# Reordering TensorE's opening and the block sums of an attention-plus-FFN kernel

## The chip, the cores and the metric

The kernel runs on one core of a Trainium2 chip. The metric is the device time of one execution in microseconds (us). Times of a kernel are the median over its executions; a profile is one execution with the hardware profiler, and its "span" runs from the first to the last instruction (mostly 1.8 to 2.0 us shorter than the device time of the same execution).

## The reference

```python
def _attn_ref(q, k, v, E, F):                      # q, k, v: 8 x 8 x 1024 x 64
    k_proj = np.einsum('ks,bhsd->bhkd', E, k)      # 64 projected positions
    v_proj = np.einsum('ks,bhsd->bhkd', F, v)
    scores = scale * np.matmul(q, k_proj.transpose(0, 1, 3, 2))
    attn = softmax(scores)                         # written out with max, exp, sum in the original
    return np.matmul(attn, v_proj)
# then, with x = the attention output as 8192 x 512:
h = x @ w_in                                       # 512 -> 2048
g = h * (1.0 / (1.0 + np.exp(-1.702 * h)))
return g @ w_out                                   # 2048 -> 512
```

## The kernel before

The 8192 rows are done in 16 blocks of 512 (two blocks for each batch). A block is a first FFN part (matmuls of line L399), a second FFN part (L423), and between their matmuls, at places named by `at(block, slot, ...)`, pieces of attention for later blocks. Batch 0 has no FFN to hide in and is done in the open, in the "opening". The parts that matter:

```python
    def v_piece(p, cp):                            # opening: v's projection of two heads
        v_ps = proj0(1, 2 * p, 2)                  # L177, 8 matmuls
        for r, t in ((LO, p % 2), (HI, 1 - p % 2)):
            cp(vx0[p][r, t, :D], v_ps[r, t])       # L203, two copies on the engine given
    ...
    def kv_out(b):                                 # after a batch's projections (L169)
        def go():
            ps = kvps.pop(b)
            k_b = att.tile([KP, H, D], BF16, name="k_b")
            nc.vector.tensor_copy(k_b, ps[LO])     # L217
            nc.sync.dma_start_transpose(out=kts[b % 2], in_=k_b...)   # L218, makes kt
            v_out(b, ps)                           # L211, two copies to vq
        return go
    ...
    def sums(h):                                   # softmax sums of block h, L296
        def go():
            d_ps = [ps_x.tile([P, TB], F32, name="x_ps") for _ in range(2)]
            ... 8 matmuls ...
            for e in range(2):
                nc.vector.reciprocal(rden[:, e, :], d_ps[e])          # L299
        return go

    def spread(h):                                 # reciprocals to DRAM, then to all partitions
        def go():
            nc.sync.dma_start(out=rdr, in_=...)                       # L306
            for e, r in enumerate((LO, HI)):
                nc.sync.dma_start(out=rbc[h][r], in_=rdr[...]...)     # L309
        return go

    def values(h, u):                              # attention's output of block h
        def go():
            n_ps = [ps_x.tile([P, TB], F32, name="x_ps") for _ in range(2)]
            ... 8 matmuls ...
            for i in range(2):                     # L331, frees the two x_ps tiles
                nc.vector.tensor_tensor(x_of(h)[...], n_ps[i], rbc[h][...], op=ALU.mult)
        return go
    ...
    at(2, 3, proj(2), kv_out(2), sums(3), spread(3))
    at(2, O + 6, proj(3), kv_out(3), scores(5, 1), sums(4), spread(4))
```

The `x_ps` tiles are four in all. `sums(4)` takes the two that `values(3, 0)` used, so it can start only when block 3's first two multiplies are done, and these need block 3's `rbc`.

The softmax here doesn't subtract the row's maximum and nothing guards it: scores larger than these inputs give would overflow.

Of the kernel before, what the change touches and what calls it, by code (L numbers as in the profile page):

```python
# [17 lines left out]
def kernel(ctx, tc, q, k, v, E, F,  # L18
                                                     moe_w_in, moe_w_out, out):
    nc = tc.nc  # L20
# [88 lines left out]
    LO, HI = slice(0, KP), slice(KP, P)  # L109
# [22 lines left out]
    def f_tile(shape, dt=F32):  # L132
        return ps_f.tile(shape, dt, name="f_ps")

    def warm(n, f=False, z=zeros):
        w_ps = f_tile([P, TB]) if f else ps_x.tile([P, TB], F32, name="x_ps")
        for _ in range(n):
            nc.tensor.matmul(w_ps, z[:, :P], z, start=True, stop=True)  # L138
# [19 lines left out]
    def eft(j, cols=slice(0, 2 * KP)):  # L158
        return efts[j // (J // 2)][:, j % (J // 2), cols]
# [4 lines left out]
    def proj(b):  # L164
        def go():
            kvps[b] = f_tile([P, H, D])
            for j in range(J):
                for e, r in enumerate((LO, HI)):
                    nc.tensor.matmul(kvps[b][r], eft(j, slice(e * KP, (e + 1) * KP)),  # L169
                                     (kt, vt)[e][b][:, :, j, :],  # L170
                                     start=(j == 0), stop=(j == J - 1))
        return go

    def proj0(e, h0, n):
        ps = f_tile([P, n, D])
        for j in range(J):
            nc.tensor.matmul(ps, ffs[:, j].rearrange("s i k -> s (i k)") if e else eft(j), (kt, vt)[e][0][:, h0:h0 + n, j, :],  # L177
                             start=(j == 0), stop=(j == J - 1))
        return ps
# [16 lines left out]
    def vx_of(b, p):  # L196
        return vx1[:, 2 * p:2 * p + 2] if b == 1 else vx0[p]

    def v_piece(p, cp):

        v_ps = proj0(1, 2 * p, 2)
        for r, t in ((LO, p % 2), (HI, 1 - p % 2)):
            cp(vx0[p][r, t, :D], v_ps[r, t])  # L203

    def v_out(b, v_ps):
        vv = v_ps[HI].rearrange("k (u x) d -> k u x d", x=4)
        for r, xs_ in ((LO, X_LO), (HI, X_HI)):
            if b == 1:
                vx = vx1[r, :, :D].rearrange("k (u x) d -> k u x d", x=4)
                nc.vector.tensor_copy(vx[:, :, xs_], vv[:, :, xs_])  # L210
            nc.vector.tensor_copy(vqs[b % 2][r].rearrange("k (u e) d -> k u e d", e=2), vv[:, :, xs_, :])  # L211

    def kv_out(b):
        def go():
            ps = kvps.pop(b)
            k_b = att.tile([KP, H, D], BF16, name="k_b")
            nc.vector.tensor_copy(k_b, ps[LO])  # L217
            nc.sync.dma_start_transpose(out=kts[b % 2], in_=k_b.rearrange("k h d -> k (h d)"))  # L218
            v_out(b, ps)
        return go  # L220
# [11 lines left out]
    def q_tr(g):  # L232
        def go():
            if 0 not in qT:
                qT[0] = att.tile([P, J, HP, P], BF16, name="qT")
            t_ps = f_tile([P, 2, HP, P], BF16)
            for jj in range(2):
                for h in range(H):
                    r = h % 2 * D
                    nc.tensor.transpose(t_ps[r:r + D, jj, h // 2, :], qt[0][:, h, 2 * g + jj, :], ident)  # L240
            nc.vector.tensor_copy(qT[0][:, 2 * g:2 * g + 2], t_ps)
        return go

    def q_dma(b, j0=0, n=J):
        def go():
            if j0 == 0:
                qT[b] = att.tile([P, J, HP, P], BF16, name="qT")
            nc.sync.dma_start_transpose(out=qT[b][:, j0:j0 + n].rearrange("r j p s -> r (j p) s"),
                                        in_=qt[b][:, j0:j0 + n].rearrange("s j h d -> s (j h d)"))
        return go  # L250
# [32 lines left out]
    def x_of(h):  # L283
        if h not in xT:
            xT[h] = att.tile([P, KC, TB], BF16, name="xT", bufs=3)
        return xT[h]

    def sums(h):


        def go():
            d_ps = [ps_x.tile([P, TB], F32, name="x_ps") for _ in range(2)]
            for p in range(HP):
                for e in range(2):
                    r = HI if (p + e) % 2 else LO
                    nc.tensor.matmul(d_ps[e][32 * p:32 * p + 32], ones[r, :32], expT[h][r, p, :], start=True, stop=True)  # L296
            rden = att.tile([P, 2, TB], F32, name="rden", bufs=1)
            for e in range(2):
                nc.vector.reciprocal(rden[:, e, :], d_ps[e])  # L299
            rdens[h] = rden  # L300
        return go

    def spread(h):
        def go():
            rdr = dram.tile([HP, 2, TB], F32, name="rdr")
            nc.sync.dma_start(out=rdr, in_=rdens.pop(h)[0:P:32])  # L306
            rbc[h] = att.tile([P, HP, TB], F32, name="rbc")
            for e, r in enumerate((LO, HI)):
                nc.sync.dma_start(out=rbc[h][r], in_=rdr[None, :, e, :].to_broadcast([D, HP, TB]))  # L309
        return go  # L310
# [30 lines left out]
    def sums0(half):  # L341
        d_ps = ps_x.tile([P, HP, 2, 2], F32, name="x_ps")
        for p in range(HP):
            for i in range(2):
                t = 2 * half + i
                nc.tensor.matmul(d_ps[:, p, i, :], expT[0][:, p, t * P:(t + 1) * P],
                                 vx_of(0, p)[:, :, D:].rearrange("r t o -> r (t o)"), start=True, stop=True)
        nc.vector.reciprocal(rd0[:, half], d_ps)

    def tok0(p, a):  # L350
        n_ps = (f_tile if a else lambda s: ps_x.tile(s, F32, name="x_ps"))([P, 2, 2, D])
        for i in range(2):
            t = 2 * a + i
            nc.tensor.matmul(n_ps[:, i].rearrange("s t d -> s (t d)"),
                             expT[0][:, p, t * P:(t + 1) * P], vx_of(0, p)[:, :, :D], start=True, stop=True)
        if p not in xs:
            xs[p] = work.tile([P, 2, 2, 2, D], BF16, name="x0_sb", bufs=4)
        nc.vector.tensor_tensor(xs[p][:, a], n_ps, rd0[:, a, p, :, :, None].to_broadcast([P, 2, 2, D]), op=ALU.mult)

    def x_tr0(p, a, n, cp):  # L360
        n_ps = ps_x.tile([P, 2 * n, P], BF16, name="x_ps")
        for t in range(2 * n):
            nc.tensor.transpose(n_ps[:, t, :], xs[p][:, a + t // 2, t % 2].rearrange("s t d -> s (t d)"), ident)
        cp(x_of(0)[:, p, a * TB // 2:(a + n) * TB // 2], n_ps.rearrange("r t s -> r (t s)"))
# [69 lines left out]
    def at(j, slot, *fs):  # L434
        fill.setdefault((j, slot), []).extend(fs)
# [7 lines left out]
    DV, AC = nc.vector.tensor_copy, nc.scalar.copy  # L443
# [7 lines left out]
    gelu_table()  # L451
    v_piece(0, DV)
    sums0(0)
    tok0(0, 0)
    v_piece(1, DV)
    tok0(1, 0)
    sums0(1)
    v_piece(2, DV)
    tok0(0, 1)
    tok0(1, 1)  # L460
    v_piece(3, AC)
    tok0(2, 0)
    tok0(2, 1)
    x_tr0(0, 0, 2, AC)
    warm(1, True)
    tok0(3, 0)
    tok0(3, 1)
    x_tr0(1, 0, 2, AC)
    warm(1, True)
    x_tr0(2, 0, 2, DV)  # L470
    x_tr0(3, 0, 1, AC)
    x_tr0(3, 1, 1, DV)
    at(0, 13, q_tr(2))
    at(0, 15, q_tr(3))
    for u in range(2):
# [2 lines left out]
    for p in range(HP):  # L478
        at(0, Q + (4, 6, 9, 11)[p], tok(1, p, 0), tok(1, p, 1))
        at(0, Q + (6, 9, 11, 12)[p], x_tr(1, p, 0), x_tr(1, p, 1))  # L480
    at(1, 1, q_dma(1, 0, JB))
    at(1, 5, proj(1), kv_out(1), q_dma(1, JB, JB))
    for u in range(2):
        at(1, O, scores(2, u, None, u > 0))
# [6 lines left out]
        at(1, O + 6, scores(3, u, None, u > 0))  # L491
    at(1, O + 6, gelu_table)
    at(1, O + 4, q_dma(2))
    at(2, 3, proj(2), kv_out(2), sums(3), spread(3))
    at(2, O, q_dma(3))
    at(2, O + 3, scores(5, 0))
    at(2, O + 6, proj(3), kv_out(3), scores(5, 1), sums(4), spread(4))
    at(2, O + 7, gelu_table)
    for b in range(4, B):
# [66 lines left out]
```

## Time and profile before

| what | number | where from |
|---|---|---|
| device time | 509.6 us (508.96 to 509.95, 3 runs) | the first runs of the kernel before |
| device time of the profiled execution | 511.27 us | its record |
| span of the profile | 509.5 us | page |
| TensorE busy | 98% of the span | page |
| first FFN matmul starts | 23.47 us | TensorE's timeline |
| first landing of a piece of k | 9.54 us | the record of transfers |
| block 3's multiplies start | 119.17 us | VectorE's timeline |
| block 5's second scores, which block 4's sums follow | 119.40 us | TensorE's timeline |

The scores at 119.40 us are `scores(5, 1)` of the line `at(2, O + 6, ...)`, so block 5's, and block 4's sums come right behind them. The prediction and the expectations call them block 4's scores; nothing in the working hangs on the name. "The scores" below are these.

How to read the lines: a timeline line is start, duration, engine, source line, operation, out<-in, shapes and a count; in brackets it has the idle time of the engine ahead of it and what ended it. A line of the table of waits is: who waited <- for what: us in total, how often, the longest. The ends of matmuls are modelled (eight sums of before, listed with 386 ns each, start and give way to FFN within 0.35 us, 93.12 to 93.47), so distances between starts are used below. TensorE waits little (98% busy), and only its waits can be won. A landing is the time at which a transfer has arrived whole; a PSUM tile (`f_ps`, `x_ps`) is what matmuls write and another engine reads. In before, a matmul that takes such a tile again is listed as waiting for the reader: `PE x_ps L296 <- DVE xT L331: 0.2, 1, 0.2`.

### The profile page before, as it was taken

The page shows a single profiled execution, that of the slowest core. Times are in us where ns is not written, and L with a number is a line of the kernel's source. Part 1 is how long each engine was busy: PE and PEld are TensorE (multiplying, and loading weights), DVE is VectorE, ACT ScalarE, POOL GpSimd, SP SyncE. Part 2 cuts the span into 40 slices and gives each one's busy share as a digit, 9 for nine tenths or more (in the row PEclk, how much of TensorE's full clock was granted, in tenths as well). Part 3 has the DMA queues.
Part 4 walks back from the last instruction along what each step waited for, and adds up shares of the span by engine and source line. Part 5 has one row for each costly group of instructions (what it writes and reads, how often), then busy time and mean ns, then how long its engine had stood idle before and what let it go on. Part 6 is the DMA issues. An engine that isn't in the chain of part 4 may idle for free.

```text
span 509.5 us, 7096 instructions
## 1 busy us (share of the span) xinstructions
PE 501.5 (98%) x3034; PEld 227.2 (45%) x3034; DVE 156.2 (31%) x208; ACT 261.3 (51%) x426; POOL 77.8 (15%) x97
## 2 busy tenths in 40 slices
PE   7899999999999999999999999999999999999997
PEld 3644445444444444444444444444444444444444
DVE  4513204606261623216161331616214161611000
ACT  1565473654637355471746637374563737244351
POOL 6452150510600510041000510000000000000000
PEclk9999999999999999999999999999999999999999
DMA  9999999999799999499938979090603205050202
GB/s 164 200 202 207 195 160 175 213 202 136 137 216 268 132 153 205 130 153 93 239 55 214 104 116 233 13 241 1 172 0 74 93 7 160 1 167 0 84 0 82
DMA packets 124711, 68.76 MB, mean 135 GB/s; under 512 B 90580, under 2 KB 115540, under 8 KB 122760
## 3 DMA queue, kind: packets, MB, share of 16 engines
q0 software_dynamic: 83376, 29.37, 52.5%
q1 hardware_dynamic: 41224, 38.69, 30.8%
q8 instruction: 23, 0.38, 0.3%
q10 hardware_dynamic: 80, 0.26, 0.2%
q14 instruction: 8, 0.07, 0.0%
HBM read 72.88 MB, written 16.99 MB: 176 GB/s over the span
## 4 chain that ended last, share of the span: by engine, by line
PE 90%; DMA 6%; DVE 2%; POOL 1%; issue 0%; SPq 0%; ACT 0%; DVEq 0%; POOLq 0%
PE f_ps L399 41%; PE f_ps L423 41%; DMA v_sb<-in_v_dram 3%; DMA rbc<-rdr 2%; PE f_ps L169 2%; PE f_ps L258 1%; DVE rden L299 1%; PE x_ps L258 1%; DMA rdr<-rden 1%; PE f_ps L415 1%; PE x_ps L296 1%; POOL k_sb L57 0%; POOL v_sb L57 0%; PE x_ps L371 0%; PE x_ps L386 0%
## 5 line engine op out<-in xcount | busy, mean ns | idle before, releaser
L423 PE MATMUL f_ps<-w_out_sb,gT 128*128 128x512 bf16 x1008 | 226.7, 379 | 0.0
L399 PE MATMUL f_ps<-xT,w_in_sb 128*128 128x512 bf16 (+1 forms) x1032 | 224.4, 377 | 0.0
L401 ACT ACTIVATE gT<-f_ps 128x512 bf16<-128x512 f32 (+1 forms) x258 | 150.4, 594 | 61.4 <-PE f_ps L399 61.1
L399 PEld LDWEIGHTS <-w_in_sb 128*128 128x128 bf16 x1032 | 100.6, 98 | 119.8 <-issue 0.6
L423 PEld LDWEIGHTS <-gT 128*128 128x128 bf16 x1008 | 95.8, 98 | 121.7 <-issue 11.6
L426 ACT COPY o_sb<-f_ps 128x512 f32<-128x512 f32 x63 | 37.0, 587 | 131.6 <-PE f_ps L423 121.8
L331 DVE TENSOR_TENSOR xT<-x_ps,rbc 128x512 bf16<-128x512 f32 x52 | 33.3, 684 | 219.2 <-PE x_ps L258 115.3
L299 DVE RECIPROCAL rden<-x_ps 128x512 f32<-128x512 f32 x26 | 85.3, 3322 | 9.2 <-PE x_ps L296 9.2
L70 POOL DMA_DIRECT2D q_sb<-in_q_dram x48 | 42.1, 901 | 152.6 <-DMA qT<-q_sb 128.2
L277 ACT ACTIVATE expT<-f_ps 128x512 bf16<-128x512 f32 (+1 forms) x54 | 28.5, 580 | 29.4 <-PE f_ps L258 29.3
L277 ACT ACT_TABLE_LOAD x13 | 16.7, 1283 | 4.7 <-PE f_ps L258 4.5
L281 ACT ACT_TABLE_LOAD x14 | 18.0, 1283 | 0.3
L57 POOL DMA_DIRECT2D k_sb<-in_k_dram x10 | 8.5, 848 | 48.4 <-PE f_ps L169 46.3
L217 DVE CAST k_b<-f_ps 64x512 bf16<-64x512 f32 x7 | 4.8, 682 | 34.9 <-PE f_ps L169 34.9
L169 PE MATMUL f_ps<-k_sb,eft 128*64 128x512 bf16 x56 | 13.4, 382 | 0.0
L169 PE MATMUL f_ps<-v_sb,eft 128*64 128x512 bf16 x56 | 13.4, 382 | 0.0
L417 DVE COPY o_sb<-f_ps 128x256 f32<-128x256 f32 (+1 forms) x2 | 0.7, 358 | 37.3 <-issue 36.9
L138 PE MATMUL x_ps<-zeros 128*128 128x512 bf16 (+1 forms) x20 | 9.2, 589 | 1.5 <-DVE zeros L115 1.5
L258 PE MATMUL x_ps<-expT,vq 64*32 64x512 bf16 x208 | 10.2, 378 | 0.0
L258 PE MATMUL f_ps<-qT,kt 64*32 64x512 bf16 x200 | 10.2, 386 | 0.0
L57 POOL DMA_DIRECT2D v_sb<-in_v_dram x11 | 9.0, 822 | 7.9 <-DMA q_sb<-in_q_dram 4.3
L169 PEld LDWEIGHTS <-eft 128*64 128x64 bf16 x112 | 5.7, 109 | 7.3 <-issue 3.0
(75 smaller groups left out, 126.5 us busy)
## 6 DMA issues: line engine op xcount, KB each, us to landing
out_dram<-o_sb SPq DMA_DIRECT2D x15, 1024.0 KB
rbc<-rdr SPq DMA_DIRECT2D x26, 512.0 KB
k_sb<-in_k_dram POOLq DMA_DIRECT2D x7, 1024.0 KB, 13.4
v_sb<-in_v_dram POOLq DMA_DIRECT2D x7, 1024.0 KB, 17.6
q_sb<-in_q_dram POOLq DMA_DIRECT2D x48, 128.0 KB, 5.8
w_in_sb<-in_moe_w_in_dram POOLq DMA_DIRECT2D x8, 256.0 KB, 11.7
w_out_sb<-in_moe_w_out_dram POOLq DMA_DIRECT2D x4, 512.0 KB, 14.7
q_even<-in_q_dram POOLq DMA_DIRECT2D x2, 512.0 KB, 11.7
```

The source lines that it names most:

```text
L57: nc.gpsimd.dma_start(out=dst[b][:, h:h + n, js:js + jn], in_=sv[:, h:h + n, js:js + jn])
L70: nc.gpsimd.dma_start(out=qt[b][:, j], in_=qv[:, j])
L169: nc.tensor.matmul(kvps[b][r], eft(j, slice(e * KP, (e + 1) * KP)), (kt, vt)[e][b][:, :, j, :], start=(j == 0), stop=(j == J - 1))
L258: nc.tensor.matmul(outs[i][r.start + c:r.start + c + w], lhsTs[i][ri, c:c + w], rhss[i][ri], start=True, stop=True)
L277: nc.scalar.activation(expT[h][:, 2 * u + i, ts], s_ps[i], AF.Exp, scale=scale)
L281: nc.scalar.preload_act_table(AF.Gelu_apprx_sigmoid)
L299: nc.vector.reciprocal(rden[:, e, :], d_ps[e])
L331: nc.vector.tensor_tensor(x_of(h)[:, 2 * u + i, :], n_ps[i], rbc[h][:, 2 * u + i, :], op=ALU.mult)
L399: nc.tensor.matmul(h_ps, w_in_sb[:, kc, fc * P:(fc + 1) * P], xT[j][:, kc, ts], start=(kc == 0), stop=(kc == KC - 1))
L401: nc.scalar.activation(gts[j][:, fc, ts], h_ps, AF.Gelu_apprx_sigmoid)
L423: nc.tensor.matmul(o_ps[n], gts[j][:, fc, n * P:(n + 1) * P], w_out_sb[:, fc, :], start=(fc == 0), stop=(fc == FC - 1))
L426: nc.scalar.copy(osb[j][:, n, :], o_ps.pop(n))
```

## The change

The intent: in the opening, TensorE shall not stand right behind a copy that it needs; in block 2, block 3's sums shall come ahead of batch 2's projections, so that their reciprocals start earlier. In before a reciprocal of 128x512 from PSUM took VectorE 3322 ns on average of 26, a multiply of the same size 684, which is why the order on VectorE matters. The diff, whole:

```diff
-    def kv_out(b):
+    def kv_out(b, cp=nc.vector.tensor_copy):
...
-            nc.vector.tensor_copy(k_b, ps[LO])
+            cp(k_b, ps[LO])
...
     v_piece(0, DV)
     sums0(0)
+    v_piece(1, DV)
     tok0(0, 0)
-    v_piece(1, DV)
+    sums0(1)
     tok0(1, 0)
-    sums0(1)
     v_piece(2, DV)
     tok0(0, 1)
     tok0(1, 1)
-    v_piece(3, AC)
+    warm(1, True)
     tok0(2, 0)
     tok0(2, 1)
     x_tr0(0, 0, 2, AC)
-    warm(1, True)
+    v_piece(3, AC)
+    x_tr0(1, 0, 2, AC)
     tok0(3, 0)
     tok0(3, 1)
-    x_tr0(1, 0, 2, AC)
     warm(1, True)
-    x_tr0(2, 0, 2, DV)
-    x_tr0(3, 0, 1, AC)
-    x_tr0(3, 1, 1, DV)
+    x_tr0(2, 0, 2, AC)
+    x_tr0(3, 0, 1, DV)
+    x_tr0(3, 1, 1, AC)
...
-    at(2, 3, proj(2), kv_out(2), sums(3), spread(3))
+    at(2, 3, sums(3), proj(2), kv_out(2, nc.scalar.copy), spread(3))
```

`DV` and `AC` are the copies of VectorE and ScalarE, `tok0` is half-block values, `x_tr0` transposes them, `warm` is a filler matmul.

## The prediction

> **What bounds the kernel now.** I read the page first, then the table of TensorE's waits over the whole span, then TensorE's timeline in the opening and around block 2, and last VectorE's and SyncE's timelines beside them. The busy line (busy us, share of the span, instructions) comes first:
>
> ```profile
> PE 501.5 (98%) x3034; PEld 227.2 (45%) x3034; DVE 156.2 (31%) x208; ACT 261.3 (51%) x426; POOL 77.8 (15%) x97
> ```
>
> TensorE is busy for 98% of 509.5 us and the change removes no matmul, so it can win only idle time of TensorE. The table of waits (us in total, times, longest) shows how little of it the change can touch:
>
> ```profile
> PE x_ps L354 <- DVE vx L203: 0.9, 2, 0.6
> PE f_ps L177 <- DMA v_sb<-in_v_dram: 0.5, 1, 0.5
> PE x_ps L296 <- DVE xT L331: 0.2, 1, 0.2
> ```
>
> The first row is what the change's title speaks of: half-block values (L354) waiting for the copies of v's projections (L203). Two later rows matter as much. In TensorE's timeline of the opening (start, duration, what, and in brackets the idle time before) they stand so:
>
> ```profile
> 16.93 0.62 PE L177 MATMUL f_ps<-v_sb,ffs 128*128 128x128 bf16 x8
> ...
> 18.10 0.29 PE L354 MATMUL x_ps<-vx,expT 128*128 128x128 bf16 x2 [0.37 <-DVE vx L203]
> ...
> 19.40 0.29 PE L354 MATMUL x_ps<-vx,expT 128*128 128x128 bf16 x2 [0.56 <-DVE vx L203]
> ...
> 21.09 0.62 PE L177 MATMUL f_ps<-v_sb,ffs 128*128 128x128 bf16 x8 [0.52 <-DMA v_sb<-in_v_dram]
> ...
> 22.23 0.27 PE L354 MATMUL x_ps<-vx,expT 128*128 128x128 bf16 x2
> ...
> 23.47 10.64 PE L399 MATMUL f_ps<-xT,w_in_sb 128*128 128x256 bf16 x56
> ```
>
> After both copy waits TensorE still stands 0.52 us at 21.09 for the last quarter of v, whose transfer lands at 21.04. So the opening is set by that landing and by what must follow it, and the two copy waits lie before it, in slack. ScalarE and VectorE show what follows:
>
> ```profile
> 21.75 0.43 ACT L203 CAST vx<-f_ps 64x64 bf16<-64x64 f32 x2 [1.96 <-PE f_ps L177]
> ```
> ```profile
> 22.88 0.41 DVE L358 TENSOR_TENSOR x_sb<-f_ps,rd 128x256 bf16<-128x256 f32 x1
> ```
>
> The third row of the table is block 4's sums, at the end of block 2's second FFN part:
>
> ```profile
> 119.40 0.41 PE L258 MATMUL f_ps<-qT,kt 64*32 64x512 bf16 x8
> 119.92 0.37 PE L296 MATMUL x_ps<-expT,ones 64*32 64x512 bf16 x1
> 120.52 0.41 PE L296 MATMUL x_ps<-expT,ones 64*32 64x512 bf16 x7 [0.22 <-DVE xT L331]
> 120.86 1.90 PE L423 MATMUL f_ps<-w_out_sb,gT 128*128 128x512 bf16 x8
> ```
>
> Elsewhere eight scores are followed after 0.23 us by eight sums (138.22 to 138.45), and eight sums after 0.35 us by FFN matmuls (93.12 to 93.47). Here 119.40 to 120.86 is 1.46 us where 0.58 would do: **0.88 us** are lost, though the table lists 0.2. The sums need PSUM tiles that block 3's multiplies (L331) still hold, and those came late:
>
> ```profile
> 94.88 6.57 DVE L299 RECIPROCAL rden<-x_ps 128x512 f32<-128x512 f32 x2
> 119.17 2.48 DVE L331 TENSOR_TENSOR xT<-x_ps,rbc 128x512 bf16<-128x512 f32 x4 [17.73 <-DMA rbc<-rdr]
> ```
> ```profile
> 101.47 0.62 SPq L306 DMA_DIRECT2D rdr<-rden  x1
> 106.16 1.32 SPq L309 DMA_DIRECT2D rbc<-rdr  x2
> ```
>
> Two reciprocals until 101.44, a store to DRAM, 4.7 us to its landing, two broadcasts landing at 116.8 and 119.08, then the multiplies.
>
> [...] the second sums matmul starts 0.60 us after the first and only 0.22 is called idle, so I work from starts. [...] Here eight 128-column projections take 16.93 to 17.38, 56 ns each, and FFN groups of four follow every 0.86 us; moving them changes no cost. [...] The store of 16 KB took 4.7 us here and 1.9 at 129.78[...].
>
> **The change, part by part.** *1. Projections, sums and half-block values.* A projection can be used 1.17 us after its first matmul with VectorE's copies (16.93 to 18.10; 18.23 to 19.40), 1.14 with ScalarE's (21.09 to 22.23). The pieces on TensorE: projection 0.45, sums 0.21, a pair of values matmuls 0.12, four transposes 0.23, a filler matmul 0.23. Replayed in the new order: v0 at 16.93; sums 17.38; v1 17.59 to 18.04; values of pair 0 at 18.10, a wait of 0.06; second sums, whose last tile needs the exponential that ends at 18.49, until 18.60; values of pair 1 when v1's copies are done, at 18.87 (VectorE runs them 18.35 to 18.81, behind a reciprocal). v2 then starts at 18.99 instead of 19.73: **0.74 us gained at this point**, and v2's copies, queued behind two multiplies and a reciprocal on VectorE, end at about 20.24. Pair 2's values go at 20.30, its transposes of pair 0 by 20.9, and then TensorE meets the landing at 21.04. The whole 0.74 ends as more waiting; v3 starts at 21.09 as before.
>
> From there the necessary chain is v3, copies 21.75 to 22.18, pair 3's values 22.23, two multiplies (22.54 to 22.96, 22.88 to 23.29), transposes at 23.35, FFN at 23.47. In the old order the 0.68 us between v3's end (21.55) and 22.23 were filled exactly: values of pair 2 0.22, transposes 0.23, filler 0.23. The new order has moved these three ahead of v3 and leaves one set of transposes, 0.23: 0.45 us of open wait for the copies replace useful work, and pair 3 starts no sooner. Then values 0.22, filler 0.23, transposes of pair 2 from 22.68, pair 3's first half at 23.02 and second half at 23.35 after its multiply, FFN 23.47: the same. What the copies' new engines change is small: pair 2's copy ends at about 23.68 instead of 23.74, so the third FFN matmul starts at 23.73 instead of 23.79. Gain **0.06 us**.
>
> *2. Block 3's sums ahead of batch 2's projections.* The sums matmuls move from 93.12 to 91.28, and the reciprocals need not stand behind the copies of k and v (93.26 to 94.88). With 0.45 us from last matmul to reader (92.81 to 93.26) the reciprocals start at 91.31 + 0.45 = 91.76 instead of 94.88: 3.12 us earlier, and end at 98.33. The store lands 4.7 us later at 103.0, the broadcasts' second one at 103.7 + 12.2 = 115.9. To be in time for the sums at 119.63 it must land by 119.63 - 0.05 - 1.29 (first two multiplies, 119.17 to 120.46) = 118.3. It does by 2.4 us. So the **0.88 us** are gained whole.
>
> *3. k's copy to ScalarE.* ScalarE is idle from 91.98 to 94.54 in this stage and the copy (0.6 us, at about 93.6) fits; its transfer of kt moves from 93.97 to about 94.2, read at 105.66. Nothing on the path.
>
> Sum: 509.6 - 0.88 - 0.06 = 508.7 us.
>
> **Rivals.** *A: the copies' waits are worth what the table says.* Then 0.9 in the opening, perhaps also the 0.5, and with 0.88 the time is about 507.3 to 507.8. For it: the title's intent. Against: the landing at 21.04 does not move, since GpSimd issues it at 7.06 whatever TensorE does. *B: the held PSUM tile.* v's copies of batch 2 now stand behind the reciprocals, so the projections' tile is held until 98.33 + 0.87 = 99.2 instead of 94.84. Were it the fourth FFN group's, due at 93.47 + 3 x 0.863 = 96.1, TensorE would lose about 3 us (512). The instruction order of the built program speaks against it: the VectorE wait has moved from the fourth group after the projections to the ninth, due at 100.4, 1.2 us later than needed. *C: the broadcast is bound by the loads around it.* Loads of the next batch land from 104.7 to 122.3 in the same engines. If the store lands only when k's load is done, about 105, 1 us is left of the 3.1, enough by a hair; if nothing of it is left, the gain is 0.06 us (509.5). *D: the last quarter of v lands earlier in runs without this delay* (the earlier quarters came 1.3 us apart, this one 2.4). Then the old order could start FFN some 0.3 us sooner, and the new one, tied by its longer VectorE queue, only 0.1: about 508.9.
>
> **Range and chances.** I give the whole 0.88 about four chances in five. The three runs before spread over 1 us (508.96 to 509.95), which is as large as the gain, so the range is 507.9 to 509.5. Two per cent is 10 us; nothing here comes near it, either way: faster 0.01, same 0.98, slower 0.01.
>
> **What would show it.** Right: the waits table loses the L296 row; the store of block 3 issues near 98.4, its multiplies start near 116, and from block 4's scores to the next FFN takes 0.6 us; FFN starts within 0.1 us of 23.47; at pair 3's values a wait of about 0.4 for ScalarE's copies appears, beside waits for VectorE's of about 0.3 and 0.4 earlier. Wrong: FFN starting before 23.2 with the landing unmoved (A); an FFN matmul near 100 waiting for v's copies (B); the multiplies still after 118.3 (C).

Why the store took 4.7 us at one place and 1.9 at the other is not shown. Two things that the argument needs are in the traces. VectorE's copies did wait for the two reciprocals ahead of them: in after, ScalarE reads batch 2's projections from 92.19 us, but VectorE's copies from the same tile start only at 96.94, behind the reciprocals of 90.34 to 96.91. Loads and broadcast (rival C) were under way in the same DMA engines at the same time: from 101 to 120 us of before, the profile's packet times of the loads' queue come to 154.6% of the 16 engines' span, those of the queue with the broadcast to 26.7%, and 2.52 and 1.07 MB were moved.

## The result, and the profile after

The changed kernel took 508.97 us (median of 4 runs, 508.77 to 510.0); the kernel before, in 4 runs, 509.3 us. The ratio is 0.9996, interval 0.9978 to 1.0014. A ratio is the mean time of one kernel's runs over that of the other's of the same rounds, so it is not quite the ratio of the medians quoted. By that count the two are the same.

The profiles seem to say more: the span fell from 509.5 to 507.2 us, by 2.31 us. It is worth taking apart. Page of the changed kernel, busy line:

```profile
PE 500.9 (99%) x3034; PEld 227.2 (45%) x3034; DVE 155.0 (31%) x206; ACT 262.5 (52%) x428; POOL 77.8 (15%) x97
```

Its table of TensorE's waits, the last three rows:

```profile
PE f_ps L149 <- ACT ef_sb L143: 0.4, 1, 0.4
PE x_ps L354 <- ACT vx L203: 0.3, 1, 0.3
PE f_ps L258 <- DMA kt<-k_b: 0.2, 1, 0.2
```

The wait of the sums (L296) is gone from the table, as are the waits for VectorE's copies. (By starts one of these is left: a filler matmul of 0.23 us stands at 18.14, and pair 2's values follow it only at 18.62, a wait of 0.25 us.) In their place is one for ScalarE's copies, and a new one for kt. TensorE's timeline of the opening, changed kernel:

```profile
15.51 0.62 PE L177 MATMUL f_ps<-v_sb,ffs 128*128 128x128 bf16 x8
...
17.46 0.61 PE L177 MATMUL f_ps<-v_sb,ffs 128*128 128x128 bf16 x8
...
19.47 0.61 PE L177 MATMUL f_ps<-v_sb,ffs 128*128 128x128 bf16 x8
...
20.60 0.27 PE L354 MATMUL x_ps<-vx,expT 128*128 128x128 bf16 x2 [0.29 <-ACT vx L203]
...
21.84 2.37 PE L399 MATMUL f_ps<-xT,w_in_sb 128*128 128x256 bf16 x18
```

The five marks are the projections of v's first, third and last quarters, pair 3's values, and FFN. In the kernel before v's first projection came at 16.93; here it comes at 15.51, although nothing ahead of it was changed. The reason is the first piece of k, which landed at 8.12 us here and at 9.54 there; from that landing to v's first projection it takes 7.39 us in both. That alone is 1.42 of the 2.31 us.

TensorE, VectorE and SyncE around block 2, changed kernel:

```profile
117.99 0.41 PE L258 MATMUL f_ps<-qT,kt 64*32 64x512 bf16 x8
118.21 0.40 PE L296 MATMUL x_ps<-expT,ones 64*32 64x512 bf16 x8
118.55 1.90 PE L423 MATMUL f_ps<-w_out_sb,gT 128*128 128x512 bf16 x8
```
```profile
90.34 6.57 DVE L299 RECIPROCAL rden<-x_ps 128x512 f32<-128x512 f32 x2 [5.83 <-PE x_ps L296]
...
113.99 2.48 DVE L331 TENSOR_TENSOR xT<-x_ps,rbc 128x512 bf16<-128x512 f32 x4 [16.19 <-DMA rbc<-rdr]
```
```profile
96.94 0.63 SPq L306 DMA_DIRECT2D rdr<-rden  x1
102.01 1.32 SPq L309 DMA_DIRECT2D rbc<-rdr  x2
```

From the scores to the FFN matmul it now takes 0.56 us, and the multiplies start 4.0 us ahead of the scores (113.99 against 117.99) instead of 0.23.

So the 2.31 us are: 1.42 from the first landing; 0.21 more until FFN starts (16.93 to 23.47 is 6.55 without rounding, 15.51 to 21.84 is 6.34); 0.07 in the first FFN matmuls; then 0.28 lost, because the scores of attention block 2, at 71.20 in FFN block 1, had to wait for kt; then 0.89 won in FFN block 2. Together that is 2.31. From block 3 on both profiles run the same 380.24 us from FFN to FFN. Whether those parts belong to the change is what the experiments had to tell.

### The profile page after: what moved, and what is told of

It reads as the page before. It is cut to its first block, busy times and chain, and to the rows that moved or that the text cites. A ratio compares the mean times of both kernels' runs of the same rounds, so it can differ in the third digit from the quotient of the medians.

```text
span 507.2 us, 7095 instructions
## 1 busy us (share of the span) xinstructions
PE 500.9 (99%) x3034; PEld 227.2 (45%) x3034; DVE 155.0 (31%) x206; ACT 262.5 (52%) x428; POOL 77.8 (15%) x97
## 4 chain that ended last, share of the span: by engine, by line
PE 93%; DMA 4%; POOL 1%; DVE 0%; issue 0%; ACT 0%; POOLq 0%
PE f_ps L423 43%; PE f_ps L399 42%; PE f_ps L169 3%; DMA v_sb<-in_v_dram 2%; DMA kt<-k_b 2%; PE f_ps L258 2%; PE x_ps L258 1%; PE f_ps L415 1%; PE x_ps L296 1%; POOL k_sb L57 0%; POOL v_sb L57 0%; PE x_ps L371 0%; PE x_ps L386 0%; PE f_ps L240 0%; POOL q_even L57 0%
## 5 line engine op out<-in xcount | busy, mean ns | idle before, releaser
L423 PEld LDWEIGHTS <-gT 128*128 128x128 bf16 x1008 | 95.9, 98 | 121.7 <-issue 11.8
L169 PE MATMUL f_ps<-k_sb,eft 128*64 128x512 bf16 x56 | 13.4, 382 | 0.0
L169 PE MATMUL f_ps<-v_sb,eft 128*64 128x512 bf16 x56 | 13.4, 382 | 0.0
```

Of the source, the lines that this page charges most:

```text
L169: nc.tensor.matmul(kvps[b][r], eft(j, slice(e * KP, (e + 1) * KP)), (kt, vt)[e][b][:, :, j, :], start=(j == 0), stop=(j == J - 1))
L423: nc.tensor.matmul(o_ps[n], gts[j][:, fc, n * P:(n + 1) * P], w_out_sb[:, fc, :], start=(fc == 0), stop=(fc == FC - 1))
```

## The experiments

Twelve different kernels were run, the first two of them twice. Each run left a profile, fourteen in all, and every profile from block 3's first FFN matmul to the last FFN block takes the same 380.24 us, so all differences lie before it, but for the end of tuned. The readings from starts and landings, in us:

| profile | order of opening / block 2 | first k lands | v's first projection to FFN | v's last landing to FFN | multiplies after (+) or ahead (-) of the scores | block 2, FFN to FFN |
|---|---|---|---|---|---|---|
| before | old / old | 9.54 | 6.55 | 2.43 | -0.23 | 34.86 |
| before_again | old / old | 8.67 | 6.20 | 3.25 | -1.36 | 33.97 |
| after | new / new | 8.12 | 6.34 | 2.41 | -3.99 | 33.97 |
| after_again | new / new | 8.68 | 6.36 | 2.41 | -4.04 | 33.97 |
| open_only | new / old | 8.16 | 6.33 | 2.41 | -1.50 | 33.97 |
| block2_only | old / new | 8.36 | 6.42 | 2.43 | -4.40 | 33.97 |
| v3_no_wait_old | old / old | 9.50 | 6.20 | - | +0.06 | 35.15 |
| v3_no_wait_new | new / new | 8.50 | 6.10 | - | -4.61 | 33.97 |
| late_old | old / old, delayed | 9.10 | 6.65 | 2.43 | +1.21 | 36.30 |
| late_new | new / new, delayed | 8.30 | 6.36 | 2.41 | -2.44 | 33.97 |
| k_act_only | old / k's copy only | 8.20 | 6.56 | 2.43 | -1.59 | 33.97 |
| sums_first_dve | old / sums only | 8.41 | 6.55 | 2.43 | -0.98 | 34.11 |
| no_q3_old | old / old, one load less | 8.35 | 6.46 | 2.43 | -4.07 | 33.97 |
| tuned | tuned / new | 9.24 | 6.11 | 2.25 | -3.90 | 33.97 |

### The same kernels again: before_again, after_again

No edit.

> The kernel before, unchanged, for a second profile and for the noise of the comparison. Theory (first landing is chance): the ratio is 1.000 within 0.001; the first piece of k lands somewhere between 8.1 and 9.6 us as the executions fall, so the spans may differ by over 1 us with no change of code; from the first projection of v to the first FFN matmul it takes 6.5 us as before, and from block 4's scores (the ones followed by sums) to the next FFN matmul 1.46 us, both independent of the landing. Rival (the change moved the first landing): the first piece of k lands at 9.5 us again, as in the first profile of before.

> The changed kernel, a second profile. Theory: from v's first projection to FFN 6.3 us and from block 4's scores to the FFN matmul 0.56 us, as in its first profile; the first piece of k may land at 8.1 or at 9.5. A wait of the first scores of block 2 for kt of 0.2 to 0.3 us comes back if it is the price of the earlier opening, and is absent in some profiles if it is chance of the transfers. Ratio to before 0.998 (0.9 us of 509), hard to tell from 1. Rival (the change moved the first landing): k lands at 8.1 again, and the ratio is 0.9955.

before_again: 509.39 us, ratio 1.001 (0.9996 to 1.0024). after_again: 508.61 us, ratio 0.9992 (0.9979 to 1.0004), against 509.14 us for the kernel before in these rounds. The profile of the unchanged kernel came out at 507.3 us, as short as the changed kernel's. TensorE and VectorE in it, around block 4's sums:

```profile
118.07 0.41 PE L258 MATMUL f_ps<-qT,kt 64*32 64x512 bf16 x8
118.30 0.40 PE L296 MATMUL x_ps<-expT,ones 64*32 64x512 bf16 x8
118.63 1.90 PE L423 MATMUL f_ps<-w_out_sb,gT 128*128 128x512 bf16 x7
```
```profile
116.71 2.48 DVE L331 TENSOR_TENSOR xT<-x_ps,rbc 128x512 bf16<-128x512 f32 x4 [16.59 <-DMA rbc<-rdr]
```

In this execution of the old order the multiplies began 1.36 us ahead of the scores, and the sums waited for nothing: 0.56 us from scores to FFN. My expectation of 1.46 us failed. **The wait of the first profile is not in every execution of the kernel before.** The first landing of k moved too, from 9.54 to 8.67 without any edit, so that part of the theory (chance) holds. The opening took 6.20 us where I expected 6.5, because here v's last quarter landed 1.26 us after the third instead of 2.41. The kt wait did not come back in after_again, nor in open_only, v3_no_wait_new, late_new or tuned, so it is no steady price of the earlier opening.

### Each part alone: open_only, block2_only

open_only has the opening's lines of the diff only, block2_only the other three edits only.

> The opening's part of the change alone. Theory: v's first projection to FFN 6.3 us against 6.54, of which 0.06 by the copies' new engines and the rest chance of the last landing of v; block 4's scores to FFN still 1.46 us; ratio 0.9995 to 1.000. Rival (the copy waits of 0.93 us are won): 5.6 us and ratio 0.998.

> Block 3's sums ahead of batch 2's projections, and k's copy on ScalarE, alone. Theory: opening as before (6.5 us), block 4's scores to FFN 0.56 us, so 0.9 us are won here: ratio 0.998. Rival (the multiplies came in time only because the loads were 1.4 us ahead in that profile): the multiplies start at 117 or later, and less than 0.5 us is won.

open_only: 509.56 us, ratio 1.0003 (0.9991 to 1.0016). block2_only: 509.05 us, ratio 1.0003 (0.999 to 1.0015). Times cannot tell them from the kernel before. The profiles can. The opening's order gives 6.33 us and, from v's last landing to FFN, 2.41 us where the old order needs 2.43. Block 2's order moves the multiplies to 4.40 us ahead of the scores. With the old order of block 2, open_only had no wait there either (-1.50), against my expectation of 1.46 us from scores to FFN.

### The margin, made visible: late_old, late_new

```diff
             rden = att.tile([P, 2, TB], F32, name="rden", bufs=1)
+            if h == 3:
+                nc.vector.reciprocal(rden[:, 0, :TB // 2], d_ps[0][:, :TB // 2])
             for e in range(2):
                 nc.vector.reciprocal(rden[:, e, :], d_ps[e])
```

Both kernels have it: one further reciprocal of half the columns, whose result is overwritten.

> The kernel before with one more reciprocal of 128x256 (about 1.7 us of VectorE) ahead of block 3's two, so that its broadcast and multiplies come 1.7 us later; the result is unchanged. In two profiles with the old order of block 2 the multiplies began 1.36 and 1.51 us ahead of block 4's scores and cost nothing, in one 0.23 us ahead and 0.88 us were lost. Theory (a thin margin of the old order): here they begin about 0.2 to 0.4 us after the scores, and from the scores to the FFN matmul it takes 0.56 + 1.3 to 1.6 = 1.9 to 2.2 us instead of 0.56 (2.9 to 3.1 where the transfers are as late as in the first profile); ratio to before about 1.002 to 1.003. Rival (the sums waited for something else in the first profile): 0.56 us here too and ratio 1.000.

> The changed kernel with the same additional reciprocal. Its multiplies began 4.0 us ahead of block 4's scores, so they now begin about 2.3 us ahead. Theory: from the scores to the FFN matmul still 0.56 us, no time is lost, ratio to before 0.999; the v copies behind the reciprocals end at about 98.8 and the ninth FFN group after the projections, which takes their PSUM tile, waits for nothing or 0.2 us at most. Rival: the held PSUM tile costs over 0.5 us.

late_old: 511.97 us, ratio 1.005 (1.0029 to 1.0071). late_new: 509.24 us, ratio 0.9997 (0.9979 to 1.0016). Table of waits and VectorE's timeline of late_old, then VectorE's of late_new (the added line moves the source lines: L301 are the block's reciprocals, L333 the multiplies):

```profile
PE x_ps L296 <- DVE xT L333: 1.8, 2, 1.5
```
```profile
120.26 2.48 DVE L333 TENSOR_TENSOR xT<-x_ps,rbc 128x512 bf16<-128x512 f32 x4 [17.38 <-DMA rbc<-rdr]
```
```profile
115.47 2.48 DVE L333 TENSOR_TENSOR xT<-x_ps,rbc 128x512 bf16<-128x512 f32 x4 [15.96 <-DMA rbc<-rdr]
```

The added reciprocal is listed with 1.76 us in both, and the block's own start 1.79 us after it (94.53 to 96.32, 90.26 to 92.05). The same 1.79 us of delay cost the old order 2.33 us in block 2 (36.30 against 33.97) and the new order nothing. That was more than the 1.3 to 1.6 us expected of a usual execution, since the multiplies came 1.21 us after the scores; from the scores to FFN it took 2.89 us, at the edge of the 2.9 to 3.1 expected where the transfers are late. Here the times show it too: all six executions of late_old (511.45 us or more) are slower than all six of late_new (511.13 us or less). So the sums do wait for these multiplies, and the change has moved a margin.

In these profiles the margin follows a plain rule. The sums could start 0.22 us after the scores (117.99 to 118.21 in after); the first two multiplies need 1.29 us (119.17 to 120.46 in before), and the sums that wait for them start about 0.05 later (120.52). So the loss should be 1.12 us plus the column "multiplies after the scores" where that is positive: 0.89 for -0.23, 1.18 for +0.06, 0.14 for -0.98, 2.33 for +1.21, nothing below -1.12. Block 2's lengths over 33.97 are 0.89, 1.18, 0.14 and 2.33 in these profiles, and none in the ten others.

In late_new the held PSUM tile went to the eleventh FFN group after the projections, not the ninth: by the semaphores in the traces, the matmul that must wait for v's copies stands at 100.62 us, and at 98.97 in the changed kernel. No wait for it appeared.

### Without the last landing of v: v3_no_wait_old, v3_no_wait_new

```diff
-        v_ps = proj0(1, 2 * p, 2)
+        v_ps = proj0(1, 2 * min(p, 2), 2)
```

Wrong (relative error 0.28 in both): the last projection reads v's third quarter, which has landed long before.

> Wrong result on purpose: the last projection of v in the opening reads the third quarter of v instead of the fourth, so nothing waits for the fourth's landing; order as before. Theory (the landing hides the copy waits): from the first projection of v to the FFN matmul 6.1 to 6.25 us, as in the one profile where the last quarter landed early (6.20), against 6.55 and 6.42 where it was late. Rival (the copy waits bound the opening): 6.5.

> Wrong result on purpose: the same with the new order. Theory: 6.2 to 6.3 us, so slightly slower than the old order without the landing, because pair 2's copies stand on VectorE behind two multiplies and a reciprocal, and ScalarE's copy for pair 0 stands ahead of pair 3's. Rival (the new order has fewer waits, and the landing alone hides it): 5.6 to 5.9 us.

TensorE's timeline, first the old order, then the new (v's first projection and the first FFN matmul):

```profile
16.89 0.62 PE L177 MATMUL f_ps<-v_sb,ffs 128*128 128x128 bf16 x8
...
23.09 1.15 PE L399 MATMUL f_ps<-xT,w_in_sb 128*128 128x256 bf16 x9
```
```profile
15.89 0.62 PE L177 MATMUL f_ps<-v_sb,ffs 128*128 128x128 bf16 x8
...
22.00 2.37 PE L399 MATMUL f_ps<-xT,w_in_sb 128*128 128x256 bf16 x18
```

6.20 us against 6.10. With the landing out of the way the old order still lists both copy waits (0.9 us together), and the new one lists only 0.3 for ScalarE's; yet the new order is only 0.10 us shorter. So the copy waits are not what bounds the opening even then. What does is only read from the traces: VectorE works without a gap from 19.68 us until after FFN's start in the old order, and in the new one the chain of pair 3 stands behind the last projection (19.59, pair 3's values at 20.75, FFN at 22.00). The sign I expected (the new order slightly slower) was wrong by some 0.1 us. v3_no_wait_old also gave a second execution of the old block 2 with the long wait: multiplies 0.06 us after the scores, 1.18 us lost. Its one time was 511.07 us.

### Parts of block 2: sums_first_dve, k_act_only

```diff
 # sums_first_dve
-    at(2, 3, proj(2), kv_out(2), sums(3), spread(3))
+    at(2, 3, sums(3), proj(2), kv_out(2), spread(3))
 # k_act_only (kv_out with the argument cp, as in the change)
-    at(2, 3, proj(2), kv_out(2), sums(3), spread(3))
+    at(2, 3, proj(2), kv_out(2, nc.scalar.copy), sums(3), spread(3))
```

> The kernel before with block 3's sums ahead of batch 2's projections, but k's copy left on VectorE, where it now stands behind both reciprocals. Theory (the copy on ScalarE is what makes the move affordable): k's copy ends about 6 us later, its transfer to kt issues near 98 to 99 and lands near 105 to 106, so block 4's first scores (104 to 105) wait 0.5 to 2 us for kt, and the small store behind it is held too, so the multiplies begin less than 2.5 us ahead of block 4's second scores; block 2 takes 0.5 to 2 us longer than 33.97. Rival (the copy's engine does not matter): 33.97, multiplies 4 us ahead.

> The kernel before with only batch 2's copy of k moved to ScalarE; the sums stay behind the projections. Theory: the reciprocals begin about 0.7 us earlier instead of 3.1, so the multiplies begin 2.0 to 2.2 us ahead of block 4's scores in an execution like the two undisturbed ones (0.9 in one like the first): 33.97 us for block 2, or up to 0.3 more. Rival (the margin does not follow the reciprocals, as the transfers set it): 1.4 us ahead.

sums_first_dve: 509.42 us, ratio 0.9998 (0.9982 to 1.0013); k_act_only: 509.12 us, ratio 0.9995 (0.9981 to 1.0008). SyncE and VectorE of sums_first_dve, then VectorE of k_act_only:

```profile
97.76 1.18 SPq L218 DMA_TRANSPOSE kt<-k_b  x1
98.99 0.63 SPq L306 DMA_DIRECT2D rdr<-rden  x1
```
```profile
92.56 0.87 DVE L211 CAST vq<-f_ps 64x256 bf16<-64x256 f32 x2 [7.95 <-ACT k_b L217]
93.45 6.57 DVE L299 RECIPROCAL rden<-x_ps 128x512 f32<-128x512 f32 x2
```

With the sums first but k's copy on VectorE, kt's transfer issues at 97.76 and the store of the reciprocals stands behind it, at 98.99 instead of about 97 (96.94 in after). The multiplies began 0.98 us ahead of the scores, no more than the old order's 1.36 in before_again, and block 2 lost 0.14 us, not the 0.5 to 2 expected. kt itself landed at 103.96, just ahead of the scores at 104.54, so the wait for kt that I expected did not come. With k's copy alone on ScalarE the reciprocals did not move forward by 0.7 us: VectorE's copies of v are listed as released by ScalarE's copy of k, which reads the same PSUM tile, so the reciprocals came only 0.1 us earlier than in before_again (93.45 against 93.55). No run shows whether that wait is needed. The margin was 1.59 us, hardly more than without it. So in these profiles, one of each, neither edit alone gives the margin that the pair gives. What the sums alone would give is less sure: counted from block 2's first FFN matmul, the store issued 1.36 us earlier than in the kernel before (12.38 against 13.74), but the broadcast then took 13.13 us from its issue to the multiplies, as long as in the executions of the old order that lost time.

### What delays the broadcast: no_q3_old

```diff
-            if what == "q":
+            if what == "q" and b == 3:
+                qt[3] = qt[1]
+            elif what == "q":
                 load_q(b)
```

It computes batch 3 with batch 1's q. It passed the comparison with the reference all the same, within its tolerance.

> Wrong result on purpose: the kernel before without the load of batch 3's q, which runs beside block 3's broadcast (batch 1's q is read in its place). Theory (the store and the broadcast share the transfer engines with that load): from the issue of the broadcast to the multiplies 8 to 9.5 us instead of 11.8 to 13.4, so the multiplies begin 3 us or more ahead of block 4's scores and block 2 takes 33.97 us. Rival (the broadcast's own length sets it): 11.8 us or more as before.

One time, 509.25 us. SyncE's timeline, then VectorE's (source lines from the edit on are two higher here: L311 is the broadcast, L333 the multiplies, L250 the transpose of q):

```profile
104.73 1.32 SPq L311 DMA_DIRECT2D rbc<-rdr  x2
106.16 9.17 SPq L250 DMA_TRANSPOSE qT<-q_sb  x1
```

```profile
114.04 2.49 DVE L333 TENSOR_TENSOR xT<-x_ps,rbc 128x512 bf16<-128x512 f32 x4 [13.88 <-DMA rbc<-rdr]
```

The broadcast issued at 104.73, so it took 9.3 us to the multiplies instead of 11.8 to 13.4 with the old order. The multiplies began 4.07 us ahead of the scores with the old order of block 2. In this one profile, then, the margin comes back without any reordering once the load of q beside the broadcast is gone: that load, next to the late start of the reciprocals, seems to be what makes the margin thin. The edit changed one thing more: with no load to wait for, the transpose of q issued right behind the broadcast, at 106.16 instead of 122.45, so the load's effect was not measured quite alone.

### A version meant to beat both: tuned

```diff
+        if isinstance(cp, tuple):
+            for c, r, t in zip(cp, (LO, HI), (p % 2, 1 - p % 2)):
+                v_ps = proj0(1, 2 * p + t, 1)
+                c(vx0[p][r, t, :D], v_ps[r, 0])
+            return
...
-    v_piece(3, AC)
+    v_piece(3, (AC, DV))
     x_tr0(1, 0, 2, AC)
+    x_tr0(2, 0, 2, AC)
     tok0(3, 0)
     tok0(3, 1)
     warm(1, True)
-    x_tr0(2, 0, 2, AC)
```

> A version meant to beat both: the changed kernel, with the last projection of v split by head into two PSUM tiles whose copies run side by side on ScalarE and VectorE, and pair 2's transposes moved ahead of pair 3's values into the wait there. Theory (the chain from the last landing of v sets the opening): landing to FFN 2.2 us instead of 2.41, pair 3's values about 0.95 us after the projection's first matmul instead of 1.13, no wait for ScalarE's copies over 0.1 us; the ratio to the changed kernel is 0.9996, too small for the timing to show. Rival (the chain is set by the multiplies and copies behind it): 2.4 us still.

TensorE's timeline of tuned (pair 3's values are L359 here, FFN L404):

```profile
20.53 0.63 PE L177 MATMUL f_ps<-v_sb,ffs 128*128 128x64 bf16 x16
...
21.48 0.29 PE L359 MATMUL x_ps<-vx,expT 128*128 128x128 bf16 x2
...
22.73 3.64 PE L404 MATMUL f_ps<-xT,w_in_sb 128*128 128x256 bf16 x23
```

The chain shortened as expected: 0.95 us from the projection to pair 3's values, 2.25 us from landing to FFN. The two copies start 0.18 us apart, ScalarE's at 21.01 (0.21 us) and VectorE's at 21.19 (0.23 us). The times did not follow: 510.15 us against 509.64 for the kernel before, ratio 1.0012 (1.0 to 1.0025). In its profile the first k landed late (9.24), and from the last FFN block to the end it took 7.18 us instead of 6.67, with the last three output transfers issued over 2.43 us instead of 1.90. Why, the trace does not show. No round ran it beside the changed kernel; it did not beat the kernel before, so it gives no reason to prefer it.

## Why the prediction was right, point by point

**The time and the range.** 508.7 us was predicted and 508.97 measured, 508.61 in the second set of rounds; the range held both. It also holds the kernel before's own 509.3 and 509.14 us, so it would have held had the change done nothing: that the number came out near is in part luck, and the mechanism has to be judged from the profiles. Against the kernel before of the same rounds the medians differ by 0.33 and 0.53 us where 0.94 was predicted, and neither ratio is clear of 1.

**Step 1, the opening, 0.06 us.** Right in the mechanism. v's third projection started 1.96 us after the first instead of 2.80 (17.46 against 15.51; 19.73 against 16.93). None of it reached FFN: the pieces moved ahead of the last projection and the wait for pair 2's copies filled it, and the last projection still started right behind its landing (19.47 after 19.43; 21.09 after 21.04). From that landing to FFN it took 2.41 us instead of 2.43, and the first FFN matmuls lost 0.07 less to late copies (47.32 against 47.25 us from the first FFN matmul to block 1's second part): 0.09 us in all. This is not chance of two profiles: six with the old opening and a late last landing of v have 2.43 and 47.32 us, the four with the new one 2.41 and 47.25 or 47.26. The wait for ScalarE's copies at pair 3's values appeared as described, listed with 0.29 us; by starts, 20.14 (the end of the transposes' slots) to 20.60, it is the 0.45 predicted. Rival A (0.9 us from the copy waits) is refuted by open_only (2.41 us against 2.43) and by v3_no_wait_old and v3_no_wait_new. Rival D had the early landing right, 6.20 us in before_again, but not its sign: without the landing the new order was 0.10 us quicker, not slower.

**Step 2, block 3's sums, 0.88 us.** The mechanism was right, and in the profile of after the gain is 0.89 us against that of before. The multiplies were put near 116.0, that is 3.4 us ahead of the scores of the first profile, and came 4.0 ahead. Measured from the scores, the store issued 3.12 us earlier (21.05 us ahead of them, 96.94 to 117.99, against 17.93, 101.47 to 119.40), which is the shift worked out. (The prediction's landing of the second broadcast, 119.08, is 119.05 by the trace's semaphores; the sum does not change.) **What failed is the size, as a term of the sum: I took the wait of one execution for the wait of all.** In four profiles with the old order of block 2 untouched the loss was 0.89 (before), 0 (before_again), 0 (open_only) and 1.18 us (v3_no_wait_old). In six with the new order, one of them delayed on purpose, it was 0. The sum took 0.88 us from 509.6, the median of three executions of which none was as slow as the profiled one (511.27 us). Both profiles with the wait are of slow executions (511.27 and 511.07 us), and of 29 timed executions of the kernel before whose spans are on record one reached 509.3 us; the others took 506.9 to 508.8, more than half of them 507.5 or less. So the first profile was not a typical execution. What the change saves on average is not shown: the times (0.33 and 0.53 us less, 0.09 in block2_only) are too noisy to say.

**Step 3, k's copy on ScalarE.** I called it off the path, and it is. But step 2 leans on it: sums_first_dve, without it, had the store held behind kt's transfer, and in its one profile lost 0.14 us in block 2. I had not worked that out.

**Rival B** (the held PSUM tile) did not come: FFN runs from 92.05 to 102.42 without a wait, 10.37 us, as from 93.47 to 103.83 before. **Rival C** (loads around the broadcast) was not needed against the forecast, but the one profile of no_q3_old suggests that it names a reason for the thin margin.

**A reading that was wrong.** I treated the 1 us between the three runs of before as noise. Two parts of it now have names: the first piece of k landed anywhere from 8.12 to 9.54 us in fourteen profiles (its issue starts at 1.25 in both before and after), and the sums of block 4 waited in some executions only. That a large part of the 2.31 us between the two first profiles has nothing to do with the change could not be read from these two profiles alone.

**What stays open.** Why the broadcast takes 1.1 to 1.6 us longer in some executions of the old order (13.02 and 13.41 us from issue to multiplies, against 11.84 and 11.93). How often that happens, and so what the change is worth on average. The two undelayed profiles with the wait are also the two with the latest first landing of k (9.50 and 9.54), which is a coincidence of two, not a cause shown. And why tuned took longer.

## What to carry to other kernels

Before a wait in one profile is put into a forecast at full size, compare the device time of the profiled execution with the other times, and profile the same kernel again: a wait at the end of a chain of transfers can be there in one execution and gone in the next (here 0.89 us in before, none in before_again), and what the reorder really moved here is its margin (multiplies 1.36 us ahead of the scores in before_again, 4.04 in after_again), which a delay put in on purpose (1.79 us) made visible. The waits in front of copies (0.9 us) were worth next to nothing here (0.09 us), while a later landing set the pace; read what comes next on the same engine before counting it. Moving work ahead of other work on a queue may need a second, harmless looking edit, here one copy to another engine: without it, in one profile, the store issued at 98.99 us instead of 96.94, behind the transfer that was now late, and most of the margin was gone (0.98 us instead of 4).
